# Linear attention and a hard-swish layer on one core: the last output tile split by columns into two banks, the first pair of values loaded like the other pairs

## The chip, the cores and the metric

The kernel runs on one core of a Trainium2 chip. A core has TensorE (PE; its weight loads are shown as PEld), VectorE (DVE), ScalarE (ACT), GpSimd (POOL) and SyncE (SP). The metric is the device time of one execution in microseconds; the time before is the median of 4 runs.

## The reference

For 8 batches of 8 heads, 1024 positions and head size 64, keys and values are first projected along the sequence to 64 rows, then ordinary attention is taken over these, and the result goes through a layer of two matrix products with a hard-swish between them.

```
k_proj = einsum('ks,bhsd->bhkd', E, k);  v_proj = einsum('ks,bhsd->bhkd', F, v)
attn   = softmax(q @ k_proj^T / sqrt(64));  x = (attn @ v_proj) as [8192, 512]
h = x @ w_in;   g = h * clip(h + 3, 0, 6) / 6;   out = g @ w_out
```

w_in is 512 x 2048, w_out is 2048 x 512; everything comes in and goes out as f32.

## The kernel before

Matmuls take bf16. DMAs issued by GpSimd (queue q0 of the profile) convert f32 to bf16 on the way; those issued by SyncE (q1) and ScalarE (q10) do not convert.

**The start** (lines 72 to 153). E and F are loaded as f32 by SyncE and ScalarE (lines 73, 74). Behind them on the same two queues, lines 76 to 79 load the values of heads 0 and 1 of batch 0 as f32, 256 KB each, into two buffers of the pool "r". GpSimd issues, in this order: for each of four pairs of heads of batch 0 the keys (line 106) and the first half of the queries (line 102); the values of pairs 1, 2 and 3 (lines 113, 114); two casts of the f32 values of pair 0 to bf16 (lines 115, 116); the seven pieces of w_in (lines 126 to 131); the second half of the queries; the four pieces of w_out (line 135); and the keys, values and queries of batch 1 (line 136). Meanwhile TensorE multiplies ones (line 89), then turns E and F (line 147) into e_t and f_t (lines 149, 151).

**The first block** (class First, lines 318 to 452) handles batch 0 pair by pair: project the keys of a pair (line 329), transpose its queries (line 357), scores of the pair before (line 370), transpose the projected keys (line 338), with exponentials and reciprocals on ScalarE (lines 166, 397, 403) between them. After the fourth pair come the value projections of the four pairs (line 345) with the products (lines 377, 406). Then the long run begins.

**The long run.** For each batch and each half of 512 positions (t), 16 groups of four matmuls (first_group, line 457, a piece fo of w_in each) fill a bank, which ScalarE and VectorE turn into g (lines 462, 463). Four groups of 16 matmuls (second_group, line 477) multiply 128 positions (c) of g by w_out into one bank, of four that rotate (pmm). The result is copied to an output buffer of four that rotate (line 491) and sent by SyncE (line 492). Attention of the next batch is worked in between.

**The last tile** (batch 7, t = 1, c = 3; lines 483 to 490): one bank of 512 columns after 16 matmuls; VectorE copies the left 256 columns, then ScalarE the right 256; SyncE sends the left half, ScalarE the right. Both halves lie in one bank and one output buffer.

The order on each engine is the order of the program text; nothing is rearranged.

Of the kernel before, what the change touches and what calls it, by code (L numbers as in the profile page):

```python
# [8 lines left out]
f32 = mybir.dt.float32  # L9
# [6 lines left out]
def kernel(  # L16
# [11 lines left out]
    nc = tc.nc  # L28
    B, H, S, D = q.shape
    KP = E.shape[0]  # L30
    d_model = H * D
    d_ff = moe_w_in.shape[1]
    scale = 1.0 / (D ** 0.5)
    P = 128
    SO = S // P
    KO = d_model // P
    FO = d_ff // P
    TOK = 512
    NB = S // TOK
    SB = SO // NB  # L40
    HT = TOK // 2

    kqv_dram = {
        "k": k.rearrange("b h (si so) d -> b si h so d", so=SO),
        "v": v.rearrange("b h (si so) d -> b si h so d", so=SO),
        "q": q.rearrange("b h (si so) d -> b si h so d", so=SO),
    }
# [10 lines left out]
    rpool = ctx.enter_context(tc.tile_pool(name="r", bufs=4))  # L58
    opool = ctx.enter_context(tc.tile_pool(name="o", bufs=4))
# [5 lines left out]
    def pmm():  # L65
        return ps_mm.tile([P, TOK], f32, tag="mm", name="mm")
# [5 lines left out]
    ef_f32 = consts.tile([P, S], f32, name="ef_f32")  # L72
    nc.sync.dma_start(out=ef_f32[:KP], in_=E)
    nc.scalar.dma_start(out=ef_f32[KP:], in_=F)

    v_f32 = []
    for a, queue in enumerate((nc.sync, nc.scalar)):
        v_f32.append(rpool.tile([P, TOK], f32, tag="r", name="r").rearrange("p (s d) -> p s d", s=SO))
        queue.dma_start(out=v_f32[a], in_=kqv_dram["v"][0][:, a])
    nc.scalar.preload_act_table_set("natural_log_exp_and_others")  # L80
    ones = consts.tile([P, TOK], bf16, name="ones")
    nc.vector.memset(ones, 1.0)  # L82
# [10 lines left out]
    def raw_tile(name):  # L93
        return kqv_pool.tile([P, H, SO, D], bf16, tag=name, name=name)


    kqv = {0: {n: raw_tile(n) for n in ("k", "q", "v")}}
# [6 lines left out]
    def load_pair(n, j):  # L104
        hs = slice(2 * j, 2 * j + 2)
        nc.gpsimd.dma_start(out=kqv[0][n][:, hs], in_=kqv_dram[n][0][:, hs])  # L106

    for j in range(KO):
        load_pair("k", j)
        load_q0(0, slice(2 * j, 2 * j + 2))  # L110
        if j == 0:
            make_identity(nc, ident)
    for j in range(1, KO):
        load_pair("v", j)
    for a in range(2):
        nc.gpsimd.tensor_copy(kqv[0]["v"][:, a], v_f32[a])

    def load_kqv(b, order="qkv"):
        kqv[b] = {}
# [5 lines left out]
    w_out_sb = consts.tile([P, FO, d_model], bf16, name="w_out_sb")  # L125
# [7 lines left out]
    for i in range(SB):  # L133
        c = slice(i * FO // SB, (i + 1) * FO // SB)
# [335 lines left out]
    def out_rows(b, t, c):  # L470
        return out_v[b, :, SB * t + 2 * (c % 2) + c // 2, :]


    def second_group(b, t, g, c, copy=None):
        o_ps = pmm()
        for fo in range(FO):
            nc.tensor.matmul(o_ps, g[:, fo, c * P:(c + 1) * P], w_out_sb[:, fo, :],  # L477
                             start=(fo == 0), stop=(fo == FO - 1))
            if fo % SB == SB - 1:
                yield  # L480
        o_sb = opool.tile([P, d_model], f32, tag="o_sb", name="o_sb")
        o_dst = out_rows(b, t, c)
        if (b, t, c) == (B - 1, NB - 1, SB - 1):

            half = slice(0, d_model // 2), slice(d_model // 2, d_model)
            nc.vector.tensor_copy(o_sb[:, half[0]], o_ps[:, half[0]])  # L486
            nc.scalar.copy(o_sb[:, half[1]], o_ps[:, half[1]])
            nc.sync.dma_start(out=o_dst[:, half[0]], in_=o_sb[:, half[0]])
            nc.scalar.dma_start(out=o_dst[:, half[1]], in_=o_sb[:, half[1]])
            return  # L490
        (copy or nc.scalar.copy)(o_sb, o_ps)  # L491
        nc.sync.dma_start(out=o_dst, in_=o_sb)

# [7 lines left out]
    def g_tile():  # L501
        return gpool.tile([P, FO, TOK], bf16, tag="g", name="g")
# [7 lines left out]
    g = [g_tile(), g_tile()]  # L510
# [17 lines left out]
    ahead.xT = x_next  # L528
    ahead = ahead.steps(PLAN)
    rows = [second_group(0, 0, g[0], c) for c in range(SB)]  # L530
    for i in range(SB + 1):
        for c in range(SB - 1):
# [12 lines left out]
    for c in range(SB):  # L545
        for _ in second_group(0, 1, g[1], c, nc.vector.tensor_copy):
            next(ahead, None)
# [8 lines left out]
    for b in range(1, B):  # L556
# [4 lines left out]
        for t in range(NB):  # L561
            if b == 1 and t == 1:
                qT_dma[3] = q_transposed(3)
            g = g_tile()
            for fo in range(FO):
                first_group(xT, t, g, fo)
                if later:
                    later.pop(0)()
                if b > 1 and t == 0 and fo == 5 and third:
                    qT_dma[b + 2] = q_transposed(b + 2)  # L570
                if b == 1 and t == 0 and fo == 10:
                    second.project()
                    second.keys_out()
                    later += [second.turn, *(lambda a=a: second.values_out(a) for a in range(2))]
                if not behind or fo % SB < SB - 1:
                    continue
                if b + 1 == B or n == 4:
                    whole(second_group(*behind[0], fo // SB))
                    continue
                rows = second_group(*behind[0], fo // SB, nc.vector.tensor_copy)  # L580
                if n < 3:
                    next(rows)
                    next(rows)
                    rest = second.visit(n, third, later)
                    whole(rows)
                else:
                    whole(rows)
                    rest = second.visit(n, third, later)
                rest()
                n += 1  # L590
# [34 lines left out]
```

The softmax here doesn't subtract the row's maximum and nothing guards it: scores larger than these inputs give would overflow.

## Time and profile before

| | us |
|---|---|
| median of 4 runs | 511.7 (511.42 to 512.46) |
| the profiled execution, whole | 512.46 |
| its span in the trace | 510.6 |
| first key projection (line 329) starts | 8.87 |
| first value projection (line 345) starts | 17.34 |
| long run (line 457) without a break from | 22.05 |
| last matmul ends | 506.62 |
| last DMA issued | 507.56 |

Lines of the chain show start, length and what ran. Lines of the transfers by queue show the queue, its number of packets, MB written, and the time of its packets as a share of 16 engines' time in the window asked for; packets that overlap can make it more than 100%. In other lines, x is a count, and a name in brackets after an arrow is what ended a wait.

TensorE's granted clock was 0.998 of full speed over the span.

### The profile page before, as it was taken

The page shows a single profiled execution, that of the slowest core. Times are in us where ns is not written, and L with a number is a line of the kernel's source. Part 1 is how long each engine was busy: PE and PEld are TensorE (multiplying, and loading weights), DVE is VectorE, ACT ScalarE, POOL GpSimd, SP SyncE. Part 2 cuts the span into 40 slices and gives each one's busy share as a digit, 9 for nine tenths or more (in the row PEclk, how much of TensorE's full clock was granted, in tenths as well). Part 3 has the DMA queues.
Part 4 walks back from the last instruction along what each step waited for, and adds up shares of the span by engine and source line. Part 5 has one row for each costly group of instructions (what it writes and reads, how often), then busy time and mean ns, then how long its engine had stood idle before and what let it go on. Part 6 is the DMA issues. An engine that isn't in the chain of part 4 may idle for free.

```text
span 510.6 us, 7165 instructions
## 1 busy us (share of the span) xinstructions
PE 501.5 (98%) x2802; PEld 224.8 (44%) x2802; DVE 257.9 (51%) x401; ACT 274.4 (54%) x493; POOL 38.3 (8%) x58
## 2 busy tenths in 40 slices
PE   7999999999999999999999999999999999999996
PEld 3544444444344444444444444444444444444442
DVE  2582836865655734657434753457434563334420
ACT  2656476567576445764456644674447654444431
POOL 7710020020010200002000020000000000000000
PEclk9999999999999999999999999999999999999999
DMA  9999999599299393515915189421110111101112
GB/s 189 199 205 207 198 158 234 98 151 178 95 177 211 69 215 84 125 41 83 226 53 105 50 139 172 101 64 33 42 41 22 41 42 42 43 21 42 41 47 78
DMA packets 74226, 55.65 MB, mean 109 GB/s; under 512 B 35536, under 2 KB 65744, under 8 KB 74192
## 3 DMA queue, kind: packets, MB, share of 16 engines
q0 software_dynamic: 31680, 29.10, 36.3%
q1 hardware_dynamic: 42144, 25.43, 19.1%
q10 hardware_dynamic: 368, 0.66, 0.5%
q8 instruction: 22, 0.36, 0.3%
q14 instruction: 12, 0.10, 0.1%
HBM read 59.24 MB, written 16.78 MB: 149 GB/s over the span
## 4 chain that ended last, share of the span: by engine, by line
PE 96%; DMA 2%; POOL 1%; DVE 1%; ACT 0%; issue 0%; DVEq 0%; POOLq 0%
PE mm L477 44%; PE mm L457 43%; PE at L188 3%; DMA k<-in_k_dram 2%; PE at L234 1%; PE mm L234 1%; PE at L216 1%; PE at L377 0%; PE at L345 0%; PE mm L216 0%; POOL q L102 0%; DVE kp L194 0%; PE at L357 0%; PE mm L377 0%; POOL k L106 0%
## 5 line engine op out<-in xcount | busy, mean ns | idle before, releaser
L463 DVE SCALAR_TENSOR_TENSOR g<-r,mm 128x512 bf16<-128x512 f32 x256 | 174.0, 687 | 131.6 <-ACT r L462 130.1
L477 PE MATMUL mm<-w_out_sb,g 128*128 128x512 bf16 x1024 | 234.7, 379 | 0.0
L457 PE MATMUL mm<-xT,w_in_sb 128*128 128x512 bf16 x1024 | 231.1, 379 | 1.3 <-DVE xT L253 1.2
L462 ACT ACTIVATE r<-mm 128x512 f32<-128x512 f32 x256 | 152.9, 599 | 75.5 <-PE mm L457 74.1
L457 PEld LDWEIGHTS <-w_in_sb 128*128 128x128 bf16 x1024 | 99.4, 98 | 123.4 <-issue 5.5
L477 PEld LDWEIGHTS <-g 128*128 128x128 bf16 x1024 | 97.9, 98 | 121.5 <-issue 7.2
L491 ACT COPY o_sb<-mm 128x512 f32<-128x512 f32 x35 | 20.3, 587 | 91.5 <-PE mm L477 91.5
L491 DVE COPY o_sb<-mm 128x512 f32<-128x512 f32 x28 | 19.4, 691 | 67.2 <-PE mm L477 67.2
L166 ACT ACTIVATE rec<-mm 128x512 f32<-128x512 f32 x34 | 19.0, 595 | 34.3 <-PE mm L234 17.6
L170 ACT ACTIVATE rec<-rec 128x512 f32<-128x512 f32 x60 | 35.6, 638 | 0.0
L253 DVE TENSOR_TENSOR xT<-at,rec 128x512 bf16<-128x512 f32 x44 | 28.1, 680 | 7.0 <-ACT rec L170 7.0
L225 ACT ACTIVATE aT<-at 128x512 bf16<-128x512 f32 x44 | 23.1, 615 | 0.9 <-PE at L216 0.9
L166 ACT ACTIVATE rec<-at 128x512 f32<-128x512 f32 x30 | 17.3, 599 | 6.0 <-PE at L234 3.7
L206 POOL COPY mark<-kT 1x1 bf16<-1x1 bf16 x5 | 0.9, 177 | 210.7 <-DMA kT<-kp 210.7
L188 PE MATMUL at<-k,e_t 128*64 128x512 bf16 x56 | 13.4, 382 | 0.0
L188 PE MATMUL at<-v,f_t 128*64 128x512 bf16 x56 | 13.4, 382 | 0.0
L194 DVE CAST kp<-at 64x512 bf16<-64x512 f32 x14 | 9.0, 678 | 4.9 <-PE at L188 4.9
L225 ACT ACTIVATE aT<-mm 128x512 bf16<-128x512 f32 x12 | 6.5, 594 | 8.9 <-PE mm L216 8.9
L197 DVE CAST vp<-at 64x512 bf16<-64x512 f32 x14 | 9.7, 694 | 0.4
L89 PE MATMUL mm<-ones 128*128 128x512 bf16 x18 | 7.4, 547 | 1.5 <-DVE ones L82 1.5
L188 PEld LDWEIGHTS <-e_t 128*64 128x64 bf16 x56 | 5.6, 109 | 7.2 <-PE at L234 2.1
L486 DVE COPY o_sb<-mm 128x256 f32<-128x256 f32 x1 | 0.4, 424 | 16.0 <-PE mm L477 16.0
(63 smaller groups left out, 150.0 us busy)
## 6 DMA issues: line engine op xcount, KB each, us to landing
out_dram<-o_sb SPq DMA_DIRECT2D x63, 256.0 KB, 2.1
k<-in_k_dram POOLq DMA_DIRECT2D x7, 1024.0 KB, 15.9
v<-in_v_dram POOLq DMA_DIRECT2D x7, 1024.0 KB, 20.8
q<-in_q_dram POOLq DMA_DIRECT2D x7, 1024.0 KB, 11.0
w_out_sb<-in_moe_w_out_dram POOLq DMA_DIRECT2D x4, 512.0 KB, 17.1
k<-in_k_dram POOLq DMA_DIRECT2D x4, 256.0 KB, 7.8
w_in_sb<-in_moe_w_in_dram POOLq DMA_DIRECT2D x2, 512.0 KB, 10.9
v<-in_v_dram POOLq DMA_DIRECT2D x3, 256.0 KB, 8.1
```

The lines of the kernel that those rows point to most:

```text
L166: nc.scalar.activation(ln, den, AF.Ln)
L170: nc.scalar.activation(ln, ln, AF.Exp, scale=-1.0)
L188: nc.tensor.matmul(ps[e * KP:(e + 1) * KP], ef_t[e][:, so, :], kqv[self.b]["kv"[e]][:, :, so, :], start=(so == 0), stop=(so == SO - 1))
L197: nc.vector.tensor_copy(self.vp[a * KP:(a + 1) * KP], self.ps[KP:].rearrange("p (h d) -> p h d", d=D))
L225: nc.scalar.activation(self.aT[j][:, r].rearrange("p a n -> p (a n)"), tiles[r], AF.Exp, scale=scale)
L234: nc.tensor.matmul(tiles[t][c:c + D].rearrange("p (r n) -> p r n", r=2), stationary(r, 2 * j + a), self.aT[j][r:r + KP, :, a, :], start=Tr ...
L253: nc.vector.tensor_mul(self.xT[:, j, t, :], av[t], recs[t])
L457: nc.tensor.matmul(h_ps, w_in_sb[:, ko, fo * P:(fo + 1) * P], xT[:, ko, t, :], start=(ko == 0), stop=(ko == KO - 1))
L462: nc.scalar.activation(r, h_ps, AF.Relu, bias=0.5, scale=1.0 / 6.0)
L463: nc.vector.scalar_tensor_tensor(g[:, fo, :], r, 1.0, h_ps, op0=ALU.min, op1=ALU.mult)
L477: nc.tensor.matmul(o_ps, g[:, fo, c * P:(c + 1) * P], w_out_sb[:, fo, :], start=(fo == 0), stop=(fo == FO - 1))
L491: (copy or nc.scalar.copy)(o_sb, o_ps)
```

## The change

Two independent parts. At the start, the f32 loads of the first pair's values and the two casts go; that pair is loaded by GpSimd with conversion, like the other three, after the last queries and ahead of pair 1. At the end, the last tile's group of 16 matmuls of 512 columns becomes two groups of 16 matmuls of 256 columns, the left half first, each with a bank and an output buffer of its own; VectorE copies and SyncE sends the left, ScalarE copies and sends the right.

```diff
-    v_f32 = []
-    for a, queue in enumerate((nc.sync, nc.scalar)):
-        v_f32.append(rpool.tile([P, TOK], f32, tag="r", name="r").rearrange("p (s d) -> p s d", s=SO))
-        queue.dma_start(out=v_f32[a], in_=kqv_dram["v"][0][:, a])
...
-    for j in range(1, KO):
+    for j in range(KO):
         load_pair("v", j)
-    for a in range(2):
-        nc.gpsimd.tensor_copy(kqv[0]["v"][:, a], v_f32[a])
...
     def second_group(b, t, g, c, copy=None):
+        o_dst = out_rows(b, t, c)
+        if (b, t, c) == (B - 1, NB - 1, SB - 1):
+
+            for e, copy, dma in ((0, nc.vector.tensor_copy, nc.sync), (1, nc.scalar.copy, nc.scalar)):
+                half = slice(e * d_model // 2, (e + 1) * d_model // 2)
+                o_ps = pmm()[:, :d_model // 2]
+                for fo in range(FO):
+                    nc.tensor.matmul(o_ps, g[:, fo, c * P:(c + 1) * P], w_out_sb[:, fo, half],
+                                     start=(fo == 0), stop=(fo == FO - 1))
+                o_sb = opool.tile([P, d_model], f32, tag="o_sb", name="o_sb")[:, :d_model // 2]
+                copy(o_sb, o_ps)
+                dma.dma_start(out=o_dst[:, half], in_=o_sb)
+            return
...
-        o_dst = out_rows(b, t, c)
-        if (b, t, c) == (B - 1, NB - 1, SB - 1):
-
-            half = slice(0, d_model // 2), slice(d_model // 2, d_model)
-            nc.vector.tensor_copy(o_sb[:, half[0]], o_ps[:, half[0]])
-            nc.scalar.copy(o_sb[:, half[1]], o_ps[:, half[1]])
-            nc.sync.dma_start(out=o_dst[:, half[0]], in_=o_sb[:, half[0]])
-            nc.scalar.dma_start(out=o_dst[:, half[1]], in_=o_sb[:, half[1]])
-            return
```

## The prediction

> **What bounds the kernel now.** I read the page first: its busy times and the shares of the chain that ended last.
>
> ```profile
> PE 501.5 (98%) x2802; PEld 224.8 (44%) x2802; DVE 257.9 (51%) x401; ACT 274.4 (54%) x493; POOL 38.3 (8%) x58
> ...
> PE 96%; DMA 2%; POOL 1%; DVE 1%; ACT 0%; issue 0%; DVEq 0%; POOLq 0%
> ```
>
> TensorE is busy for 501.5 of 510.6 us, so only what stands before its long run of matmuls (the first 22 us) and after it (the last 4 us) can be won cheaply. The change touches just these two ends. Next I read the chain of work piece by piece at the front (0 to 24 us).
>
> ```profile
> 4.72 8.03 DMA k<-in_k_dram
> 12.76 0.04 issue
> 12.80 0.63 PE at L329 x8
> ...
> 15.07 0.55 ACT aT L397 x2
> ...
> 17.41 0.55 PE at L345 x8
> ```
>
> Up to 12.8 us the chain is a transfer: the third pair of keys. After that it is arithmetic. The value projections (line 345) start as soon as PE comes to them, so the chain never stands on the values. The waits say the same: "PE at L329 <- DMA k" 1.7 us in four waits, and none of PE on v. Then the transfers by queue, first from 5 to 8 us, then from 9 to 12 us.
>
> ```profile
> q0 software_dynamic: 520, 0.40, 89.3%
> q10 hardware_dynamic: 144, 0.26, 27.0%
> q1 hardware_dynamic: 13, 0.01, 0.9%
> ```
>
> ```profile
> q0 software_dynamic: 876, 0.60, 132.3%
> ```
>
> q0 is the queue that GpSimd issues to, q1 SyncE's, q10 ScalarE's; the second number is MB written. Alone, q0 writes 0.60 MB in 3 us, 0.20 MB per us. Beside the last half of the f32 values it writes only 0.40. Last, the chain at the other end, from 504 us:
>
> ```profile
> 506.70 0.43 DVE o_sb L486
> 507.14 0.02 issue
> 507.16 0.37 ACT o_sb L487
> ```
>
> The two halves of the last output tile leave one after the other: ScalarE's copy starts when VectorE's has ended, though TensorE ended at 506.62.
>
> **The tail.** Now, 16 matmuls of 512 columns take 3.45 us in the chain (216 ns apart). Then VectorE copies 0.43 us, ScalarE 0.37 us, and the last transfer is issued at 507.56 and takes 1.9 us. After the change there are 32 matmuls of 256 columns, 16 for each bank. The first half is copied by VectorE (424 ns) and sent by SyncE beside the second half's matmuls, which last about 1.75 us: hidden. VectorE has been idle for 16.0 us there and ScalarE for 3.3 us, SyncE's last issue before was at 503.8, so nothing is queued behind these waits that anybody needs. The second half's bank is one whose copy ran at 496.29, and its output buffer was sent soon after: both free. ScalarE's copy then follows TensorE directly: it starts 0.08 us after the last matmul (as VectorE's does now, 506.62 to 506.70) in place of 0.54 us after. That removes 0.46 us.
>
> What the 16 additional matmuls and weight loads cost is not in the trace, since no full 128 x 128 matmul of 256 columns stands there. From below: half of the columns at 216 ns for 512 gives 108 ns each, 32 x 108 = 3.46 us, no change. From above: eight matmuls of 128 columns with a weight load each take 0.55 us (line 345), 69 ns apart; a straight line from 69 at 128 to 216 at 512 gives 118 ns at 256, 32 x 118 = 3.78 us, 0.32 us more. I take 110 ns, near the lower end, because the row at 512 shows no overhead over the columns and the loads at 69 ns spacing are faster than 108: +0.06 us. The tail gains 0.46 - 0.06 = 0.40 us; from 0.14 to 0.46 by the bounds.
>
> Here a row and a rule differ. The mean weight load of this tile lasts 98 ns on the page (line 477). The Trainium skill, "TensorE: Matmul & The Clock Gate", section "LDWEIGHTS (loading the stationary operand)", has a load of 128 columns at 107 ns, and under "Back-to-back issue gap" 262 cycles for 256 columns, an estimated 109 ns: by it load and matmul are level, with no room, and 32 x 109 makes 3.49 us; the page also says that both set the spacing. That speaks against halving the tile; the 69 ns rows show loads overlapping better than that.
>
> **The front: what goes.** Two DMA issues (SyncE 0.57, ScalarE 0.86 us) at 1.35 us, and two GpSimd casts at 11.77 (616 ns each). ScalarE's next work is a table load at 2.24 and a cast at 5.12 that waits for F, SyncE has nothing until 48.6 us: the issues free nothing. GpSimd's next issue after the casts, the first piece of w_in, could go up 1.18 us, but its queue is full at that time (0.60 MB in 3 us), so it moves no data earlier. What counts is 0.52 MB of f32 that no longer crosses the 16 DMA engines between 4 and 8.3 us. By 4 us, E and F had been moved (q1 0.28 MB, q10 0.26 MB). Of the values, about half moved from 4 to 5 us, when q0 had hardly begun (0.01 MB by 5 us), the rest beside q0. So q0 loses 0.60 - 0.40 = 0.20 MB, 1.0 us at its own rate, and a little more up to 8.4 us, when the slower of the two landed.
>
> How much earlier the keys land (X) is the unknown of this case. Above: if q0's late start, too, is the values' doing, it starts when E and F are through, 0.9 us earlier: X = 1.9. Below: if 0.40 MB is its own slow start, X = 0. I take 1.1, what the shared stretch shows.
>
> The first key transfer is issued at 1.24 us and q0 shows 0.01 MB by 5 us. The Trainium skill, "DMA: Bandwidth & Descriptors", section "Latency and other measured facts", gives about 1 us to the first byte on this path, an estimate of 2.2 us here; by it the wait until 5 would be contention, X nearer its upper end and the front worth some 1.65 us. The trace shows 3.7 us, with E, F and the values in flight, and cannot say which.
>
> **The front: what is added.** A ninth issue on GpSimd (0.72 us, line 106) after the fourth query part, and 0.26 MB on q0 ahead of the other values: 0.26 / 0.20 = 1.31 us. Issues on this queue go about eight deep (the second pair of values is issued at 9.11, when the first keys have landed), so the extra issue takes GpSimd's time, of which only data already queued is in front. The value pair lands after the last keys (14.64 - 1.1) and queries (0.65) at 14.2 + 1.31 = 15.5 us; needed at 17.34 - 1.1 = 16.2. Hidden, with 0.7 us over.
>
> All that follows on q0 lands 1.31 - X = 0.21 us later, while TensorE wants it X earlier. Landing times are issue plus time to landing, TensorE notices about 0.08 us after. Third values: 9.83 + 8.0 = 17.83, used at 19.18, room 1.27. First w_in: 12.89 + 7.0 = 19.89, used at 21.13, room 1.16. Third w_in: 14.39 + 7.6 = 21.99, used 23.35, room 1.28. Sixth w_in: 16.95 + 10.3 = 27.25, used at 28.53, room 1.20. First w_out: 34.96, used at 36.33, room 1.29. The least is 1.16, so the gain of the front is the smaller of X and 1.16 - (1.31 - X): for X = 1.1 it is **0.95 us**, with the first w_in as the new late one. For X = 1.9 arithmetic is the limit: the key projections cannot start before e_t at 7.96 (now 8.87), and one pair needs 1.58, 1.55 and 1.65 us of PE (transfers now pace it at 1.95), so the third pair comes 1.67 us earlier at most: gain 1.67. For X = 0, 1.16 - 1.31 = 0.15 us are lost.
>
> **The sum.** -0.95 - 0.40 = -1.35 us. The profiled execution took 512.46 us (span 510.6 and 1.86 around it), the highest of the four shown; its sum is 511.11. The median is 0.76 lower, so 511.7 - 1.35 = **510.35 us**. What the measurement can tell from no change is about 0.2%, 1.02 us.
>
> **The rivals.**
> - The key queue starts earlier too (X = 1.9): front 1.67, tail 0.40, 2.07 in all: 509.6 us. For it: two hardware queues were busy all through 2 to 5 us. Against: q0 did not share the engines then, it was absent.
> - The front gives nothing, because the 0.40 MB are q0's own start (X = 0 to 0.5): -0.15 to +0.35 us gained, with the tail 0.25 to 0.75: 511.2 us, or no measurable change. For it: q0's slices from 5 to 7 us look like a ramp. Against: it is at full rate just when q10 ends.
> - The tail gives nothing (118 ns spacing, or the two copies' gap comes back elsewhere) while the front gives 0.95: 510.75 us.
> - Slower: the weight loads of the half tile are not hidden. Then a matmul is spaced 108 + 98 = 206 ns, 32 x 206 = 6.59 us, 3.14 more than now; with the front and the 0.46 us: 511.7 + 3.14 - 0.46 - 0.95 = 513.4 us. It turns the whole change slower by 1.02 us from a spacing of 184 ns on. Against it stand the 69 ns rows with weights of the same shape.
>
> **How the numbers follow.** Forecast 0.50, earlier start 0.14, front nothing 0.20, tail nothing 0.10, slower 0.06. The forecast lies over 1.02 us below in nine tenths of its cases, the tail rival in about a quarter: faster 0.45 + 0.14 + 0.02 = 0.61; slower 0.06; the rest, 0.33, the same. The range holds the forecast, most of the earlier start, and the front that gives nothing: 509.5 to 511.4.
>
> **What the changed profile would show.** q0 at about 0.6 MB from 5 to 8 us; the first key projection at 7.96 to 8.1 and the fourth at about 13.6 in place of 14.73; the run of line 457 at about 21.1 in place of 22.05, with a short wait of PE on w_in; in the tail, VectorE's copy near 505, matmuls of 256 columns 110 ns apart, and ScalarE's copy 0.08 us behind the last. I am wrong if q0 still writes 0.40 MB from 5 to 8 us, if PE waits on v, or if the spacing nears 200 ns.

## The result and the profile after

| | before | after |
|---|---|---|
| median, us | 511.71 (61 runs) | 511.04 (41 runs) |
| range, us | 511.37 to 512.79 | 510.73 to 512.35 |
| profiled execution, us | 512.46 | 510.69 |
| its span, us | 510.6 | 508.9 |

The ratio is 0.9987, interval 0.9983 to 0.9992: faster by 0.67 us, half of the 1.35 us forecast, and inside the range of 509.5 to 511.4. It is clear of no change by the interval, but less than the 1.02 us that the prediction took as the least that can be told from no change. Three executions of the whole series, of 877, 877 and 1332 us, were disturbed and stand outside the ratios.

The two profiled executions lie 1.77 us apart, the medians 0.67. The profile of before is of an execution 0.75 us above its median, that of after of one 0.35 below. What follows has to be read with that in mind.

TensorE's share of the chain is much as before (95% for 96%). From the page of the kernel after:

```profile
PE 500.4 (98%) x2818; PEld 225.7 (44%) x2818; DVE 257.8 (51%) x401; ACT 274.4 (54%) x493; POOL 37.9 (7%) x57
...
PE 95%; DMA 2%; POOL 2%; DVE 0%; issue 0%; ACT 0%; ACTq 0%; POOLq 0%
```

The chain at the front (0 to 26 us), start, length, what:

```profile
7.61 2.09 POOL v L101 x3
9.70 9.58 DMA v<-in_v_dram
19.28 0.05 issue
19.32 0.62 PE at L338 x8
19.94 0.43 PE mm L450 x2
```

It had stood on the third keys; now it stands on a transfer of values until 19.28 us, almost up to the long run. The queues from 5 to 8 us:

```profile
q0 software_dynamic: 761, 0.55, 125.4%
```

GpSimd's queue now writes 0.55 MB there in place of 0.40. It had also moved 0.15 MB from 4 to 5 us, where it had moved 0.01. The chain at the end:

```profile
501.76 3.51 PE mm L475 x32
505.27 0.03 ACTq L478
505.29 0.04 issue
505.33 0.37 ACT o_sb L478
```

The 32 half matmuls take 3.51 us, 110 ns each, and ScalarE's copy starts 0.06 us behind them, with no copy of VectorE's in between (that one ran at 503.60). From the last matmul to the issue of the last transfer it is 0.47 us (505.27 to 505.74), before 0.94 (506.62 to 507.56).

### The profile page after: what moved, and what is told of

Its sections match the earlier page's. It is cut to its first block, busy times and chain, and to the rows that moved or that the text cites. A ratio compares the mean times of both kernels' runs of the same rounds, so it can differ in the third digit from the quotient of the medians.

```text
span 508.9 us, 7190 instructions
## 1 busy us (share of the span) xinstructions
PE 500.4 (98%) x2818; PEld 225.7 (44%) x2818; DVE 257.8 (51%) x401; ACT 274.4 (54%) x493; POOL 37.9 (7%) x57
## 4 chain that ended last, share of the span: by engine, by line
PE 95%; DMA 2%; POOL 2%; DVE 0%; issue 0%; ACT 0%; ACTq 0%; POOLq 0%
PE mm L450 44%; PE mm L483 43%; PE at L181 3%; DMA v<-in_v_dram 2%; PE at L227 1%; PE mm L227 1%; PE at L209 1%; PE mm L475 1%; POOL q L97 1%; POOL k L101 1%; POOL v L101 0%; PE mm L209 0%; PE at L370 0%; DVE kp L187 0%; PE at L350 0%
## 5 line engine op out<-in xcount | busy, mean ns | idle before, releaser
L483 PE MATMUL mm<-w_out_sb,g 128*128 128x512 bf16 x1008 | 231.2, 379 | 0.0
L483 PEld LDWEIGHTS <-g 128*128 128x128 bf16 x1008 | 96.3, 98 | 119.6 <-issue 7.2
L227 PE MATMUL at<-aT,vp 64*64 64x512 bf16 x88 | 8.5, 376 | 0.0
L84 PE MATMUL mm<-ones 128*128 128x512 bf16 x18 | 6.3, 476 | 1.5 <-DVE ones L77 1.5
```

Of the source, the lines that this page charges most:

```text
L227: nc.tensor.matmul(tiles[t][c:c + D].rearrange("p (r n) -> p r n", r=2), stationary(r, 2 * j + a), self.aT[j][r:r + KP, :, a, :], start=Tr ...
```

## The experiments

Theory A, formed after the result: the tail gave its 0.40 us, and the front much less than the two profiles suggest, because in a usual execution the bytes on GpSimd's queue ahead of the last values and the first piece of w_in set its end, not the keys. Theory B: the tail gave little, the front what was forecast. Theory C: arithmetic behind the keys ends the front. Theory D, about the fetch of TensorE's instructions, came later. All runs were timed in five rounds against the kernel before on the same chip (its medians there 511.73 to 511.79 us). Line numbers in a variant are its own.

**Tail alone.** The kernel before with the new `second_group`.

> The new tail alone, the f32 loads of the first pair's values kept. Theory A (the front was mis-sized: in a usual execution it gains only some 0.3 us, because the last values now land too late): the tail gains its whole 0.40 us, 511.3 us, and in the profile ScalarE's copy starts 0.08 us behind the last matmul. Theory B (the front gains 0.6 to 0.95 us as forecast, the tail little): 511.6 to 511.7 us.

Measured: 511.39 against 511.76 us as medians, -0.37 (ratio of the executions 0.9995, 0.9986 to 1.0004). In its profile 3.51 us of half matmuls end at 507.12 and ScalarE's copy starts at 507.18. The size is theory A's, though the interval alone does not exclude nothing; the rows do: 0.47 us less from the last matmul to the last issue, 0.06 us more for the matmuls. From the last DMA's issue to the end of the execution it is 4.85 us, before 4.90: nothing of the gain is given back behind it.

**Front alone.** The kernel after with the old `second_group`.

> The first pair's values through GpSimd's queue like the others, the old tail kept. Theory A: 0.25 to 0.35 us faster, 511.4 us, and the last value pair lands near 19.3 us with TensorE waiting for it. Theory B: 0.6 to 0.95 us faster, 510.8 to 511.1 us.

Measured: 511.64 us, -0.12 (0.9996, 0.9987 to 1.0005: from 0.66 us faster to 0.26 slower). That speaks against theory B, of whose 0.6 to 0.95 us only the edge is left, and it is less than A's 0.25 to 0.35. One more thing was wrong in A: the last values landed on time at about 18.0 us, and TensorE's weight load waited for the first piece of w_in instead:

```profile
20.00 0.11 PEld L450 LDWEIGHTS <-w_in_sb 128*128 128x128 bf16 x2 [0.33 <-DMA w_in_sb<-in_moe_w_in_dram]
```

GpSimd issues about eight deep, so each of its waits ends with a landing, which it notices some 0.28 us later (in the kernel after, 19.28 and 19.56); the bracket has the length of the wait:

```profile
17.06 0.74 POOL L120 DMA_DIRECT2D w_in_sb<-in_moe_w_in_dram  x1 [0.58 <-DMA v<-in_v_dram]
18.31 0.88 POOL L97 DMA_DIRECT2D q<-in_q_dram  x1 [0.50 <-DMA v<-in_v_dram]
20.24 1.49 POOL L128 DMA_DIRECT2D w_out_sb<-in_moe_w_out_dram  x2 [1.04 <-DMA w_in_sb<-in_moe_w_in_dram]
```

Values landed in a rhythm of 1.25 to 1.31 us; then the first piece of w_in, half as large, came with a longer wait than the 0.50 before it.

One thing differs between executions whatever the kernel: the twelve filler matmuls at the start took 5.30 us here, 4.19 in the profile of the kernel after, and the first keys were projected at 7.91 in place of 7.47, in both without a wait for the keys. So up to 0.4 us between the fronts of two single profiles can be this alone.

**The kernel before again**, unchanged.

> The kernel before once more, unchanged, for a second profile: the profiled execution of before took 512.46 us, 0.75 more than the median, that of after 510.69, 0.35 less than its median. Time: no change, within 0.1 us. Theory A expects the long run of line 457 to start near 21.3 us here, 0.7 us earlier than in the first profile, so that the 1.41 us between the two first profiles is half chance. Theory B expects 22.05 us again, within 0.2, and the surplus somewhere else.

Measured: 511.72 us; the profiled execution took 511.79, near the median. TensorE's weight loads and matmuls around the start of the long run, from its timeline:

```profile
20.50 0.11 PEld L457 LDWEIGHTS <-w_in_sb 128*128 128x128 bf16 x2 [0.26 <-DMA w_in_sb<-in_moe_w_in_dram]
```

```profile
20.73 0.38 PE L457 MATMUL mm<-xT,w_in_sb 128*128 128x512 bf16 x1 [0.31 <-DVE xT L406]
21.04 0.40 PE L377 MATMUL at<-aT,vp 64*64 64x512 bf16 x2
21.38 0.82 PE L457 MATMUL mm<-xT,w_in_sb 128*128 128x512 bf16 x3
```

(This trace has records of 2750 of the 2802 matmuls. The matmul behind the first of the two loads is missing; the one at 20.73 is the next, one spacing later, and the wait put down to xT is none.) The run starts at 21.38, not 22.05, as theory A said; the first keys are projected at 8.11, not 8.87. And before the change TensorE already waits for the first piece of w_in, 0.26 us. From the first key projection to the run it is 13.18 us in the first profile, 13.27 here and 13.17 in the kernel after: what the profiles differ by at the front is how early the keys begin. From the start of the run to the last matmul it is 484.58 us here, 484.57 in the first profile, 484.63 in the kernel after: all of the difference lies in front of the run and behind the last matmul.

**One head by SyncE**, the other through GpSimd, with the new tail.

```diff
-    for a, queue in enumerate((nc.sync, nc.scalar)):
+    for a, queue in enumerate((nc.sync,)):
...
+    nc.gpsimd.dma_start(out=kqv[0]["v"][:, 1], in_=kqv_dram["v"][0][:, 1])
```

> The new tail; of the first pair only head 0 comes as f32 by SyncE, head 1 by GpSimd's queue behind the last queries. SyncE's f32 head moved from 4 to 5.4 us, mostly when GpSimd's queue was still empty. If the bytes on GpSimd's queue up to the last values set the end of the front (theory A), 0.13 MB less on it are up to 0.65 us less than in the changed kernel, minus what the f32 head takes from that queue: 510.4 to 511.0 us. If GpSimd's queue starts late because of whatever the hardware queues move (the upper bound of the forecast), the f32 head costs as much as it saves: 511.0 to 511.3 us.

Measured: 511.27 us, -0.49 (0.9989, 0.9980 to 0.9998), no better than the kernel after: the f32 head costs what it saves. GpSimd's queue moved next to nothing from 4 to 5 us (0.00 MB), 0.15 MB in the kernel after. TensorE waits 0.57 us for the last values, and its run starts at 20.89.

**The kernel after again.**

> The changed kernel once more, unchanged, as the measure for the three that stand beside it and for a second profile. Time 511.0 us, 0.5 to 0.8 us below the kernel before. The long run starts between 20.6 and 20.9 us, with TensorE waiting for the last values or the first piece of w_in.

Measured: 510.85 us, -0.94 (0.9983, 0.9974 to 0.9992). Its profile is of the execution of 1332 us and says nothing of the others, so the start of their run stays unknown. Its time is the measure for the next three, run on the same chip.

**Without the first pair's values.** The loop of line 108 begins at 1, and `vals` takes pair `max(j, 1)`.

> The changed kernel without the load of the first pair's values: the first pair is computed from the second pair's, so this load is left out of the work. Theory A (the bytes on GpSimd's queue ahead of the last values and of the first piece of w_in set the end of the front): 0.26 MB less, both land 1.3 us earlier, the waits go, the long run starts 0.4 to 0.8 us earlier: 510.2 to 510.6 us. Theory C (arithmetic on TensorE and ScalarE sets it, the keys' arrival having been the only wait that mattered): no change, 511.0 us.

Measured: 510.14 us (five executions, 509.85 to 510.54), 0.71 below the kernel after. TensorE has no wait for a DMA left in the first 30 us. Theory C, which expected no change, falls, and these 0.26 MB are on the path, as A said. With them gone arithmetic alone is left: from the first key projection to the run it takes 12.63 us (7.88 to 20.51), in the kernel after 13.17, so the waits behind the keys cost 0.54 us there.

**Without F.** The DMA of line 74 is left out, and its rows are set by VectorE.

> The changed kernel without the load of F: its rows are set to one, so the projected values are wrong sums; one hardware load of 0.26 MB less at the start. If GpSimd's queue begins late because the two hardware loads hold the DMA engines, its first bytes come at 3.1 to 3.7 us in place of 4.4 to 4.6, all landings move up 0.7 to 1.3 us, and with theory A the time falls 0.4 to 0.8 us, to 510.2 to 510.6 us. If that start is its own, nothing moves there and the time stays within 0.2 us of 511.0.

Measured: 510.36 us, -0.49. GpSimd's queue moved 0.14 MB from 2 to 4 us, where the kernel after had nothing of it: its late start is due to the hardware loads, as the rival with X = 1.9 had it. But the fourth keys were projected at 13.23 (after: 12.47), with a wait of 0.27 us for them, and the run starts at 20.66 against 20.64. The front gained nothing in the profile. Fewer bytes are not the reason: by 8 us the queue had moved 0.78 MB, in the kernel after 0.70, and by 12 us 1.52 against 1.50. Why more bytes moved brought the keys later stays open; the bytes alone, theory A's measure, do not tell when a transfer lands. What was shorter is the end: from the last DMA's issue to the end 4.54 us, in the kernel after 4.95.

**F by GpSimd**, first in its order, converted.

```diff
-    nc.scalar.dma_start(out=ef_f32[KP:], in_=F)
+    nc.gpsimd.dma_start(out=ef_raw[KP:], in_=F)
...
-    nc.vector.tensor_copy(ef_raw[:, :S // 2], ef_f32[:, :S // 2])
-    nc.scalar.copy(ef_raw[:, S // 2:], ef_f32[:, S // 2:])
+    nc.vector.tensor_copy(ef_raw[:KP, :S // 2], ef_f32[:KP, :S // 2])
+    nc.scalar.copy(ef_raw[:KP, S // 2:], ef_f32[:KP, S // 2:])
```

> The changed kernel with F loaded and converted by GpSimd's queue, first in its order, in place of the f32 load by ScalarE; nothing is left out. It puts 0.13 MB, 0.65 us, on the queue that theory A holds for the bound. If the queue can begin at 3.1 us when only E is on a hardware queue, keys, values and w_in land 0.3 to 0.6 us earlier than in the changed kernel and the time is 510.5 to 510.8 us; if its late start is its own, they land 0.65 us later and the time is 511.4 to 511.7 us.

Measured: 511.34 us, 0.49 above the kernel after, and in the profile the same short end (4.55 us): if its other executions end as early, the front lost that 0.41 us as well, about 0.9. The queue did begin early (0.14 MB from 2 to 4 us), so the time fits the second case while its reason doesn't. The 0.13 MB added are the likely reason, not shown by themselves; TensorE waits 0.85 us for the last values.

**F by SyncE**, behind E.

> The changed kernel with F issued by SyncE behind E, so that ScalarE's queue carries only the last half tile. In the two kernels without F on that queue the time from the last DMA's issue to the end was 4.54 us against 4.90 to 4.95 in the others. If an otherwise unused ScalarE queue shortens the end, 0.4 us less than the changed kernel: 510.4 to 510.7 us, with the front as before. If those two owed it to something else, 510.8 to 511.1 us and 4.9 us again.

Measured: 511.26 us, -0.47 (0.9993, 0.9984 to 1.0001); 4.97 us from the last issue to the end (its profiled execution, 512.30, lies 1.04 us above the median). So an unused ScalarE queue does not shorten the end. The two kernels with 4.54 have one hardware load in place of two at the start; why that matters 500 us later stays open.

**The first values ahead of the last keys.**

```diff
     for j in range(KO):
+        if j == KO - 1:
+            load_pair("v", 0)
         load_pair("k", j)
...
-    for j in range(KO):
+    for j in range(1, KO):
         load_pair("v", j)
```

> The changed kernel with the first pair's values moved ahead of the fourth pair's keys on GpSimd's queue: the fourth keys land 1.3 us later, the bytes ahead of the last values and of w_in stay the same. Theory A (those bytes set the end of the front, the keys have room to spare): no change, within 0.2 us of 511.0. Theory C (the keys' arrival and the arithmetic behind it set it): 0.8 to 1.3 us slower, 511.8 to 512.3 us.

Measured: 512.88 us as a median, over two kinds of execution. Four of twelve took 510.77 to 511.22 us, with a mean granted clock of 0.999 to 1.000: no change, as theory A says. Two took 512.2 at 0.997, six 513.5 to 514.1 at 0.992 or 0.993. The other kernels' executions of 509 to 515 us show 0.997 or more. The profile is of one of the six; its windows show span, length, the busy times (TensorE, its weight loads, VectorE, ScalarE, GpSimd), and TensorE's clock as the figure before the last two:

```profile
10.00:15.00 5.00, 3.34 (x39) 2.00 (x37) 2.04 (x9) 2.43 (x6) 3.50 (x5) 1.00 1.30 202
15.00:20.00 5.00, 4.68 (x38) 2.55 (x36) 1.57 (x6) 3.66 (x8) 2.42 (x4) 0.50 1.42 196
20.00:25.00 5.00, 5.00 (x35) 2.38 (x32) 3.06 (x5) 1.50 (x4) 3.87 (x5) 0.82 1.40 200
```

```profile
14.21 0.61 PE L324 MATMUL at<-k,e_t 128*64 128x128 bf16 x8 [1.55 <-DMA k<-in_k_dram]
```

TensorE waited 1.55 us for the fourth keys and then ran at half clock from 15 to 20 us. The order of the transfers is free of cost as far as bytes go, in the four; in the six it goes with a lower clock and some 3 us. That the wait is what lowers the clock is not shown. The profile of the tail alone, of an execution of 512.43 us, has the drop with no wait for keys above 0.47 us:

```profile
10.00:15.00 5.00, 4.19 (x49) 2.65 (x47) 2.61 (x10) 2.43 (x6) 4.96 (x8) 1.00 1.30 202
15.00:20.00 5.00, 4.68 (x45) 2.90 (x44) 1.57 (x5) 3.94 (x9) 2.98 (x4) 0.66 1.43 196
```

The kernel before again has the same front, was busy for 4.26 of those first 5 us, and kept 1.00. The Trainium skill, "TensorE: Matmul & The Clock Gate", section "HAM oscillation — how this bites in real kernels", warns of idle gaps above some 3.4 us. Here no idle gap was half as long and the clock fell in two profiles; the measurement decides.

**A wide first piece of w_in**: `(0, 256)` for `(0, 128), (128, 128)`.

> The changed kernel with the first two pieces of w_in (128 columns each) loaded as one of 256. The pieces of 128 columns land some 1.6 us behind their bytes, the others 0.3 to 0.6. If TensorE only waits for this first piece, the one piece lands about where the second did, at 20.3 us or up to 0.4 us sooner, and the time is the same or up to 0.3 us less; if the room behind the first piece is real, up to 0.6 us more. Theory A predicts a change of either sign of at least 0.2 us only if that piece, and not the last values, ends the front.

Measured: 511.47 us, some 0.4 to 0.6 above the kernel after (511.04; 510.85 in the other series). TensorE waits 0.74 us for the last values and then 0.62 for this piece; the run starts at 21.53. Both sit at the end of the front together.

**More TensorE instructions** (theory D). In the kernel after, the wait for the last values is out of rhythm. GpSimd's waits, then the queues from 17 to 18 us:

```profile
15.89 0.74 POOL L120 DMA_DIRECT2D w_in_sb<-in_moe_w_in_dram  x1 [0.54 <-DMA v<-in_v_dram]
17.22 0.74 POOL L120 DMA_DIRECT2D w_in_sb<-in_moe_w_in_dram  x1 [0.58 <-DMA v<-in_v_dram]
19.56 0.88 POOL L97 DMA_DIRECT2D q<-in_q_dram  x1 [1.60 <-DMA v<-in_v_dram]
```

```profile
q0 software_dynamic: 439, 0.18, 142.0%
q8 instruction: 1, 0.02, 5.9%
```

The last landing comes 1.0 us late (2.34 us after the one before it, where 1.33 and 1.28 stood). Ahead of it one instruction packet, begun near 17.2 us, occupies 5.9% of 16 engines for 1 us, that is one engine for 0.95 us. In the kernel before (second profile) the packet came at 18.4 us, after the last values (18.28), and the first piece of w_in landed 2.2 us behind these; in the first profile, with the packet at 19.6, 0.7 us behind.

```diff
-        for _ in range(n):
-            nc.tensor.matmul(ps, ones[:, :P], ones, start=True, stop=True)
+        for _ in range(2 * n):
+            nc.tensor.matmul(ps[:, :TOK // 2], ones[:, :P], ones[:, :TOK // 2], start=True, stop=True)
```

> The changed kernel with every filler matmul of 512 columns at the start made two of 256: the same TensorE time, 34 more TensorE instructions (a weight load and a matmul each time) before the value projections. In the changed kernel one instruction packet of 16 KB crosses a DMA engine for 0.95 us at 17.4 us, and the transfer that ends next (the last value pair) lands 1.1 us later than the rhythm of the others, with all that follow. Theory D (this fetch holds back one of the 16 engines, and comes when TensorE has run a certain number of instructions): the packet comes about 1.5 us earlier, near 16 us, and the late landing moves up one transfer, to the third value pair, for which TensorE then waits; time the same or up to 0.4 us more, 510.9 to 511.4 us. Rival (the late landing has another cause): it stays with the last value pair or vanishes, whatever the packet does, 510.8 to 511.1 us.

Measured: 511.06 us (0.9989, 0.9980 to 0.9998). GpSimd's waits, then the queues from 14 to 16 us:

```profile
14.51 0.74 POOL L120 DMA_DIRECT2D w_in_sb<-in_moe_w_in_dram  x1 [0.46 <-DMA v<-in_v_dram]
17.15 1.52 POOL L120 DMA_DIRECT2D w_in_sb<-in_moe_w_in_dram  x2 [1.90 <-DMA v<-in_v_dram]
19.21 0.89 POOL L97 DMA_DIRECT2D q<-in_q_dram  x1 [0.53 <-DMA v<-in_v_dram]
```

```profile
q0 software_dynamic: 411, 0.40, 121.1%
q8 instruction: 1, 0.02, 3.0%
```

The packet came some 2.3 us earlier, more than expected, and the late landing moved with it, by two transfers in place of one: it is now the second pair's values, and TensorE waits 0.50 us for these. This fits theory D and not its rival: the fetch moves with the number of TensorE instructions, and a landing behind it is late. It is not a fixed count of those already run, which stood between 109 and 131 weight loads at the packet over the thirteen profiles. In eleven of these a wait of GpSimd of 0.89 to 1.95 us, against 0.3 to 0.6 in the rhythm, ends with a landing behind the packet; in the first profile of before and in the run without F (packets at 19.6 and 17.7) none does. So the packet does not always delay a landing, and that it does so by the one engine it holds is argued, not shown. The page counts 22 such packets, and TensorE has 5604 instructions before: 255 each. The Trainium skill, "Runtime: NRT & Kernel Launch", section "Instruction fetch mechanics", has blocks of 16 KiB, 256 instructions, and calls crossing one mostly hidden. The size agrees; mostly hidden it is not here, in a front whose loads fill all 16 engines.

## Why the prediction was half right

- **The tail was right in mechanism and size.** Forecast 0.40 us from 110 ns per half matmul and 0.46 us of copy; measured 110 ns, a copy 0.06 us behind the last matmul, 0.41 us by these rows (0.47 less 0.06), and 0.37 us as a difference of medians (tail alone). The rival of unhidden weight loads fell.
- **X was too small.** Forecast 1.1 us for the keys; between the two first profiles the fourth key projection moved from 14.73 to 12.47, and from the second profile of before (13.80) by 1.33, now without a wait for the keys, so they land at least that much earlier. GpSimd's queue starts sooner without the values beside it (0.15 MB from 4 to 5 us): the premise of the rival "starts earlier", shown once more by the run without F. Its time, 509.6, did not come: early keys are not what ends the front.
- **The step that failed is the room behind the keys, "used at 21.13, room 1.16",** with nothing put down for the fetch of TensorE's instructions. Both times were read from one execution whose packet came at 19.6 us and delayed nothing. In the second profile of before the packet came at 18.4, the first piece of w_in landed at 20.47 in place of some 19.0 (by the first profile's 0.7 us behind the last values), and TensorE waited 0.26 us for it: no room at all. That the first profile had its keys 0.8 to 0.9 us later is not the reason, since use and landing move together: the last values had a room of some 1.45 us in both.
- **In the kernel after it was the last values.** A faster front brings the fetch forward onto them; they landed 1.0 us out of rhythm, and "I am wrong if PE waits on v" came true: 0.48 us. With X = 1.33 the formula "the smaller of X and 1.16 - (1.31 - X)" gives 1.18 us; less the 1.0 us it leaves an estimate of 0.2. The front gave 0.30 us if the tail's 0.37 is taken from the 0.67; alone it measured 0.12, and 0.57 by the better of the two series. It is between 0.1 and 0.6; these runs do not narrow it, and no run takes the fetch away.
- **Arithmetic's limit, "e_t at 7.96", was one execution's.** With the changed front and E and F loaded as before, the first keys were projected at 7.29 to 7.91 us, by how long the fillers took and when F landed.
- The extra issue on GpSimd and the missing casts cost and gave nothing that shows, as forecast.

No variant that computes everything beats the kernel after beyond doubt: one head by SyncE 511.27, F by SyncE 511.26, more instructions 511.06.

## What to carry to other kernels

Before a forecast below one per cent is read from a trace, set the profiled execution's own time beside the median, and read a second one: 0.67 of the 0.75 us too much sat in just the stage that the change touched, and a landing that had 1.16 us of room in one execution had none in the next. When the loads of a stage fill all DMA engines, moving one of them to another queue changes the order of landings but hardly the last one; count the bytes up to the last thing needed, but as a first guess, since in the run without F more bytes had been moved and the keys came later. An early arrival is worth only as much as the next arrival behind it.

## What the runs showed of the hardware that was not expected

- Behind one fetch of TensorE's instructions (16 KB, 0.95 us of one DMA engine) a landing on the full queue was late in eleven of thirteen profiles, by 1.0 us in the kernel after and 1.3 with more instructions; the fetch moves with the number of TensorE instructions.
- A wait of 1.55 us on the keys was followed by 0.50 of the clock over 5 us, in some executions and not in others: 510.8 or 514 us for one kernel, in step with the mean granted clock (1.000 or 0.993). A drop to 0.66 over 5 us also came without such a wait (tail alone), so its cause is open.
- GpSimd's queue shows its first bytes at 3.1 us with one hardware load beside it or with two on SyncE's queue alone, at 3.7 to 4.1 us with one each on SyncE's and ScalarE's, at 4.9 us with three and at 4.6 to 5.3 us with four.
- With one hardware load at the start in place of two, the end of the program is 0.4 us shorter. Open.
